# A two-layer linear-attention and MLP kernel: token layout of the tiles, store queues, a zero-padded block of W_down, and a new written-out order

## The chip, the cores and the metric

The kernel runs on one core of one Trainium2 chip. A core has five engines with an instruction queue each: TensorE (PE in the profile, its weight loads PEld), VectorE (DVE), ScalarE (ACT), GpSimd (POOL) and SyncE (SP). SP and ACT issue the kernel's DMAs. The metric is the device time of one execution in microseconds (us); a kernel's time is the median of its runs. Before the change that is 368.83 us, from 3 runs between 368.44 and 368.85.

## The reference, cut to what matters

Tokens S = 2048, width D = 512, H = 32 heads of Dh = 16, MLP width F = 1376, all bfloat16. The same weights serve both layers.

```python
def A(x):                       # linear attention, hedgehog feature maps
    q, k, v = split(x @ wqkv)   # each (H, S, Dh)
    pq, pk = q @ w_phi, k @ w_phi                          # 16x16 per head
    phi_q = concat(softmax(pq), softmax(-pq))              # 32 features
    phi_k = concat(softmax(pk), softmax(-pk))
    kv, z = sum_s phi_k * v, sum_s phi_k                   # per head
    o = (phi_q @ kv) / (phi_q . z + 1e-6)
    return o @ wo

def B(x):                       # gated MLP
    gate, up = x @ W_gate, x @ W_up                        # 512 -> 1376
    return (relu(gate) * up) @ W_down                      # 1376 -> 512

x = x + A(layernorm(x)); x = x + B(layernorm(x))
x = x + A(layernorm(x)); x = x + B(layernorm(x))
```

The sum over s in kv and z runs over all 2048 tokens, so no query of a layer can be finished before the last key of that layer.

## The kernel before, in words

**Tiling.** The 2048 tokens are 16 tiles of 128 tokens, one token to a partition. x stays in on-chip memory for the whole kernel, in four buffers X[c] of four tiles each (tile t is `X[t // C][:, t % C]`, C = 4). Lines 284 and 285 say which tokens make a tile:

```python
    xv = xf.rearrange("(c p i) d -> c p i d", c=C, i=C)
    ov = of.rearrange("(c p i) d -> c p i d", c=C, i=C)
```

A chunk of 512 tokens makes four tiles, and tile i of the chunk takes every fourth token, i, i + 4, and so on. Four tokens that follow each other in DRAM lie in one partition, one in each tile. Tiles 0 to 3 are loaded one by one, tiles 4 to 15 in pairs (`load_x`, L351 for all loads of the head); a load of a pair reads two adjacent tokens, 2 KB, for each partition.

**The operations.** The body of the kernel emits nothing at once. It makes 1855 operations with `op(engine, cost, due, emit, ...)`; an operation is a handful of instructions on one engine. They are numbered as they are made. Four tables at the head of the file decide the rest, and nothing is planned when the kernel is built (costs and due times are left over and unused): ORDER is the order in which the operations are emitted, a permutation of 0 to 1854, and so the order of each engine's queue; PLACE has a bit for each operation that exists in two versions (`alt`), and a 1 takes the other version (another engine, mostly); SLOTS gives the buffer of each operation that takes one; IDLE is the number of dummy matmuls ahead of each of the first five TensorE operations (`idle`, L437), beside nine of them in an operation of their own at the start. The engines run their queues on their own and wait for each other through semaphores.

**Head.** Operation 0 preloads ScalarE's table of functions, 1 loads tile 0 of x, 2 and 3 load the halves of W_v, 4 to 6 tiles 1 to 3, 7 w_phi, 8 and 9 the halves of W_k, 10 to 15 the pairs of tiles 4-5 to 14-15; 16 makes the identity matrix and the constant ones on POOL (`first_constants`). The load of x's tile 0, of w_phi and of the four weight halves can be issued by SP or ACT (`load`); W_q's halves are operations 322 and 323 on SP (L850). W_k is folded with w_phi into Wk2 before it is used: its four blocks are transposed by TensorE ("turn", L463), copied to SBUF (wT, L443 on ACT or L444 on DVE), multiplied by the block matrix Wblk ("fold", L471; Wblk is made by L419 on POOL or DVE) and copied again (W2). W_q is transposed by DMA and folded in the same way later.

**A tile through layer one's keys.** Mean and variance on VectorE (L500, L501), ln and exp on ScalarE for the inverse deviation (L508, L510), the normed tile xn on POOL (L520 and L522) or VectorE (L524), its transpose xnTA by TensorE (L490, then a copy by ACT) for tiles 0 to 3 and by a DMA of SP (L485) for the others. Then K (L581, four matmuls of 480 columns) and V (L586, four of 512) on TensorE; from K two exponentials on ScalarE (ek, L564), their sums on VectorE (sk, L591), ln and exp of these on ScalarE (L600, L603), the feature product phi on POOL or VectorE (L551); V is copied by ACT or DVE (vext, L443/L444). Features times V, kvz (L614), accumulate over the 16 tiles in one PSUM buffer.

**Queries and attention.** When the last kvz is done, VectorE makes R and Rz of it (L626, L631). Queries run beside: Q (L641), exponentials (L564), sums (sq, L646), their product (phq, L657 and L662), a transpose by a DMA of SP (fq, L666), features times R on TensorE (erq, L677), the division (L688, L691), the transpose of the result, proj (L700), and the residual resS (L704), which is added to X in place.

**MLP.** It runs in blocks of 1, 1, 2, 4, 4 and 4 tiles. A tile is centred (xc, L720), its squares are summed (ssq, L726 on ACT or L728 on DVE), and it is transposed (xnTB). F = 1376 is ten blocks of 128 and one of FR = 96: GU (L753) computes the last 96 columns of gate and up for two tiles at once, hr (DVE) and hrT, a DMA transpose by SP (L804), bring them into h; G and Up (L777) compute the ten others, with the relu on ACT (rg, L781) and the product on DVE, directly (ru, L794) or by way of a copy on ACT (L796, then hT, L785). `down` (L817) multiplies the eleven blocks of h by W_down, 128 rows for ten of them and 96 rows for the last (`h.t[:m, ...]` and `wd[:m, ...]`); the rows 96 to 127 of h's last block are zero already, since the columns 96 to 127 of hr are set to zero at the start (`hr_zero`). resB (L824, VectorE) adds the result to X in place. In layer two the last tile is done in two parts, of 384 and 128 columns. In layer one each resB is followed by the norm and the keys of layer two for the same tile, in layer two by the store of the tile, all 17 stores by SP (L890).

**The order around the change.** In before, SP and ACT issue the loads of the head in this order (@ACT marks those of ACT): x tile 0 @ACT, x 2, w_phi @ACT, W_k first half, x 1, x 4-5, W_k second half, x 3, W_v second half, W_v first half, x 6-7, x 8-9, x 12-13, W_q first half, W_q second half, then transposes and the other loads between them. The heads of the compute queues of before, with tile or block numbers:

```
ACT  x0 load, w_phi load, table, ln2, rstd2, ln0, wT0, wT1, ln1, rstd0, rstd1, xnT copy (tile 2), W2.1 ...
PE   warm, turn0, turn1, xnT2, fold1, turn2, turn3, fold0, xnT0, fold3, fold2, xnT1, V0, K0, K2, xnT3,
     K1, V2, V3, K3, V1, K4, Wq fold, K5, Wq fold, V5, kvz0 ...
SP at the end   hrT, then 13 stores: tiles 13, 3, 0, 6, 11, 1, 7, 10, 12, 8, 14, 15 (384 columns), 15 (128 columns)
```

Of the kernel before, what the change touches and what calls it, by code (L numbers as in the profile page):

```python
# [8 lines left out]
P = 128  # L9
# [3 lines left out]
F = 1376  # L13
NB = D // P
NF = 11
# [130 lines left out]
class K:  # L146
# [9 lines left out]
    "1001001010001001101010000101111000001001111100100001101100111011000011000000100000101111011100010100"  # L156
    "1001101111010010110000010110000011011001111010011101100111110011110011001111111010011101111101011001"
    "1100011011011000110101111111111101111110010101011000010100100001101000100101111100010011011001010100"
    "1010110010011111000100110101101001100101100011101100100"
)  # L160
SLOTS = (
    "0001450332111040002521331020252213134130241204554001324122142118332305232454002133223601357001146113"
    "37331110214c1029215b124e344a030f050d1609305j031g253c321b012i144h204k360a1200050401151502000212011020"
    "2400001150000020350210121400102105010002500401004005212214201851002313115213501425303231310500410142"
    "1024202011521574410443221121100401010352431312302242101240511013402460230322025003051301002510502000"
    "1042222135013132244254224011350135402481030275405k21311041150211321401210232450232222330131532542063"
    "2110112025213310385404e052f313d2459131i320j201b062b154f210c145a3509160h004d212e331g12011301020313001"
    "0124302000035011021540000124501002145001012230210000111041011030210121231001501441322200001041042225"
    "0420351321112001514214224324413412402523105223205102100110050000220551450552131532232412541321040123"
    "1130421000550542551212451342421030015034"  # L170
# [3 lines left out]
    0, 0, 0, 0, 1,  # L174
# [104 lines left out]
def kernel(  # L279
# [22 lines left out]
    def x_of(t):  # L302
        return X[t // C][:, t % C, :]
# [52 lines left out]
    def load_x(t, n, due, follow=(), eng="SP"):  # L356
        o = load(due, X[t // C][:, t % C:t % C + n, :], xv[t // C][:, t % C:t % C + n, :], n * 131072, eng, follow, t < 1)
        x_in[t:t + n] = [o] * n
# [577 lines left out]
```

## Time and profile before

| | |
|---|---|
| median of 3 runs (lowest, highest) | 368.83 us (368.44, 368.85) |
| the profiled execution | 368.89 us |
| its span, from the first instruction to the last | 367.1 us |
| instructions | 6928 |
| PE busy | 360.5 us, 98%, 2589 matmuls |
| DVE busy | 267.8 us, 73% |
| ACT busy | 188.2 us, 51% |
| POOL busy | 71.4 us, 19% |
| moved by DMA | 31.70 MB, mean 86 GB/s |

The profile is one execution, taken by the hardware profiler. Its times begin at the start of the span; 1.8 us of the execution lie around the span. In rows of instructions the first number is the start and the second the duration (both us), then the engine, the line, the operation, the tile that it writes and those it reads, shapes (partitions x elements), and in square brackets how long the engine was idle before it and what ended that wait. A row with "xN" groups N instructions that follow each other. Rows of stages have the stretch, its length, then the busy time of PE, PEld, DVE, ACT and POOL with the number of instructions, the granted TensorE clock as a share of full speed, the share of DMA engines busy, and GB/s. Engine names ending in "q" (SPq, ACTq) are the queue that issues DMAs.

### The profile page before, as it was taken

The page shows a single profiled execution, that of the slowest core. Times are in us where ns is not written, and L with a number is a line of the kernel's source. Part 1 is how long each engine was busy: PE and PEld are TensorE (multiplying, and loading weights), DVE is VectorE, ACT ScalarE, POOL GpSimd, SP SyncE. Part 2 cuts the span into 40 slices and gives each one's busy share as a digit, 9 for nine tenths or more (in the row PEclk, how much of TensorE's full clock was granted, in tenths as well). Part 3 has the DMA queues.
Part 4 walks back from the last instruction along what each step waited for, and adds up shares of the span by engine and source line. Part 5 has one row for each costly group of instructions (what it writes and reads, how often), then busy time and mean ns, then how long its engine had stood idle before and what let it go on. Part 6 is the DMA issues. An engine that isn't in the chain of part 4 may idle for free.

```text
span 367.1 us, 6928 instructions
## 1 busy us (share of the span) xinstructions
PE 360.5 (98%) x2589; PEld 199.2 (54%) x2589; DVE 267.8 (73%) x607; ACT 188.2 (51%) x530; POOL 71.4 (19%) x101
## 2 busy tenths in 40 slices
PE   8999999999999999999999999999999999999994
PEld 4445568786545444444544556776755444454442
DVE  6999999998887247958789898899756745251342
ACT  6899998361434633414883375863423441434220
POOL 6579831210010001000208363010300000000000
PEclk9999999999999999999999999999999999999999
DMA  7987776466730600041110206346652210200025
GB/s 246 214 208 203 192 163 130 90 127 134 116 71 18 131 10 3 1 100 30 29 42 3 57 4 145 45 77 147 145 119 57 63 30 0 57 2 14 0 59 173
DMA packets 92994, 31.70 MB, mean 86 GB/s; under 512 B 85184, under 2 KB 91168, under 8 KB 92960
## 3 DMA queue, kind: packets, MB, share of 16 engines
q1 hardware_dynamic: 92288, 31.11, 38.1%
q8 instruction: 20, 0.33, 0.4%
q10 hardware_dynamic: 672, 0.15, 0.2%
q14 instruction: 14, 0.11, 0.1%
HBM read 8.44 MB, written 2.10 MB: 29 GB/s over the span
## 4 chain that ended last, share of the span: by engine, by line
PE 93%; DMA 3%; DVE 2%; issue 0%; ACTq 0%; SPq 0%; ACT 0%
PE b L777 38%; PE b L817 21%; PE b L700 8%; PE b L641 7%; PE b L586 6%; PE b L581 6%; PE b L753 3%; PE q L614 2%; PE q L677 2%; DMA X<-in_A_x_dram 2%; DMA wf<-in_A_w_phi_dram 1%; DVE bstA L500 1%; PE b L490 1%; DVE sk L591 1%; DVE X L824 0%
## 5 line engine op out<-in xcount | busy, mean ns | idle before, releaser
L777 PE MATMUL b<-xnTB,wgu 128*128 128x512 bf16 (+2 forms) x960 | 150.7, 308 | 0.0
L777 PEld LDWEIGHTS <-wgu 128*128 128x128 bf16 x960 | 80.3, 98 | 57.4 <-issue 0.2
L781 ACT ACTIVATE gu<-b 128x512 bf16<-128x512 f32 (+1 forms) x82 | 47.9, 589 | 100.0 <-PE b L777 93.6
L817 PE MATMUL b<-wd,hT 128*128 128x512 bf16 (+3 forms) x363 | 84.1, 372 | 0.0
L564 ACT ACTIVATE ek<-b 128x480 bf16<-128x480 f32 x128 | 68.2, 585 | 11.4 <-PE b L641 7.0
L794 DVE TENSOR_TENSOR hT<-gu,b 128x512 bf16<-128x512 bf16 (+1 forms) x53 | 35.1, 663 | 36.3 <-PE b L777 19.8
L551 POOL TENSOR_TENSOR ek<-ek 128x480 bf16<-128x480 bf16 x40 | 39.2, 1008 | 94.2 <-ACT ek L603 93.9
L817 PEld LDWEIGHTS <-hT 128*128 128x128 bf16 (+1 forms) x363 | 34.5, 98 | 37.4
L591 DVE TENSOR_REDUCE sk<-ek 128x64 f32<-128x960 bf16 x32 | 36.1, 1143 | 1.8 <-ACT ek L564 0.9
L646 DVE TENSOR_REDUCE sq<-ek 128x64 f32<-128x960 bf16 x32 | 36.4, 1144 | 0.0
L662 POOL TENSOR_TENSOR ek<-ek 128x480 bf16<-128x480 bf16 x18 | 18.3, 1020 | 87.2 <-DVE ek L657 56.6
L700 PE MATMUL b<-wo,oT 128*128 128x512 bf16 x128 | 31.4, 379 | 0.0
L586 PE MATMUL b<-wv,xnTA 128*128 128x512 bf16 x128 | 31.4, 379 | 0.0
L824 DVE SCALAR_TENSOR_TENSOR X<-b,rsB,X 128x512 bf16<-128x512 f32 (+2 forms) x33 | 23.8, 727 | 9.0 <-PE b L817 8.6
L581 PE MATMUL b<-Wk,xnTA 128*128 128x480 bf16 x128 | 30.2, 366 | 0.0
L641 PE MATMUL b<-Wq,xnTA 128*128 128x480 bf16 x128 | 30.1, 365 | 0.0
L691 DVE TENSOR_TENSOR o<-q,rd 128x512 bf16<-128x512 f32 x32 | 22.0, 689 | 10.0 <-ACT rd L688 9.7
L785 DVE TENSOR_TENSOR hT<-gu 128x512 bf16<-128x512 bf16 x29 | 12.1, 421 | 21.0 <-ACT gu L796 21.0
L796 ACT CAST gu<-b 128x512 bf16<-128x512 f32 x29 | 17.0, 586 | 16.2 <-PE b L777 15.4
L704 DVE SCALAR_TENSOR_TENSOR X<-b,X 128x512 bf16<-128x512 f32 x32 | 22.0, 686 | 3.5 <-PE b L700 3.3
L500 DVE BATCH_NORM_STATS2 bstA<-X 128x6 f32<-128x512 bf16 x32 | 21.3, 682 | 2.1 <-DMA X<-in_A_x_dram 2.0
L700 PEld LDWEIGHTS <-oT 128*128 128x128 bf16 x128 | 12.2, 98 | 13.2
(77 smaller groups left out, 328.8 us busy)
## 6 DMA issues: line engine op xcount, KB each, us to landing
out_dram<-X SPq DMA_DIRECT2D x15, 128.0 KB, 2.2
X<-in_A_x_dram SPq DMA_DIRECT2D x6, 256.0 KB, 4.7
wgu<-in_B_W_gate_dram SPq DMA_DIRECT2D x4, 344.0 KB, 3.4
wgu<-in_B_W_up_dram SPq DMA_DIRECT2D x4, 344.0 KB, 4.0
wd<-in_B_W_down_dram SPq DMA_DIRECT2D x5, 256.0 KB, 3.9
hT<-in_A_wqkv_dram SPq DMA_DIRECT2D x4, 256.0 KB, 5.3
wv<-in_A_wqkv_dram SPq DMA_DIRECT2D x2, 256.0 KB, 4.5
wo<-in_A_wo_dram SPq DMA_DIRECT2D x4, 128.0 KB, 4.0
```

Source lines behind the costliest of these rows:

```text
L551: e.tensor_tensor(out=v[:, :, 0:DF, :], in0=v[:, :, 0:DF, :], in1=spread(ek, v, n), op=Alu.mult)
L564: nc.scalar.activation(out=pairs(ek, s)[:, :, 0:DF, :], in_=ps.t[:, 0:FW].rearrange("p (b f h) -> p b f h", h=2, f=DF), func=AF.Exp, scale ...
L581: k = op("PE", mm(4, FW), due, lambda: [nc.tensor.matmul(kp.t[:, 0:FW], lhsT=xnTA[c][:, i, b, :], rhs=Wk2[:, b, :], start=(b == 0), stop=( ...
L586: v = op("PE", mm(4, 512), due_v, lambda: [nc.tensor.matmul(vp.t[:], lhsT=xnTA[c][:, i, b, :], rhs=wv[:, b, :], start=(b == 0), stop=(b == ...
L591: a = op("DVE", SUM16, due, lambda: nc.vector.tensor_reduce(out=sk.t[:, row, :].rearrange("p (b h) -> p b h", h=2), in_=summed(pairs(ek)), ...
L641: q = op("PE", mm(4, FW), due, lambda: [nc.tensor.matmul(qp.t[:, 0:FW], lhsT=xnTA[c][:, i, b, :], rhs=Wq2[:, b, :], start=(b == 0), stop=( ...
L646: a = op("DVE", SUM16, due, lambda: nc.vector.tensor_reduce(out=sq.t[:].rearrange("p (b h) -> p b h", h=2), in_=summed(pairs(ek)), axis=AX ...
L700: a = op("PE", mm(4, 512), due + 3, lambda j=j, yp=yp: [nc.tensor.matmul(yp.t[:], lhsT=oT.t[:, j, b, :], rhs=wo[:, b, :], start=(b == 0), ...
L777: nc.tensor.matmul(ps.t[:, q * W:(q + 1) * W].rearrange("p (i t) -> p i t", t=P), lhsT=wgu[:, s, b, g * P:(g + 1) * P], rhs=xT.t[:, 0:n, b ...
L781: nc.scalar.activation(out=gu.t[:, 0, 0:cols], in_=gp.t[:, 0:cols], func=AF.Relu)
L794: nc.vector.tensor_tensor(out=h.t[:, f0 * W:f0 * W + cols], in0=gu.t[:, 0, 0:cols], in1=up.t[:, 0:cols], op=Alu.mult)
L817: nc.tensor.matmul(yp.t[:, 0:c1 - c0], lhsT=h.t[:m, f * W + i * P:f * W + (i + 1) * P], rhs=wd[:m, f, c0:c1], start=(f == 0), stop=(f == N ...
```

## The change

Four edits of the body, and new tables.

```diff
-    xv = xf.rearrange("(c p i) d -> c p i d", c=C, i=C)
-    ov = of.rearrange("(c p i) d -> c p i d", c=C, i=C)
+    xv = xf.rearrange("(t p) d -> p t d", p=P)
+    ov = of.rearrange("(t p) d -> p t d", p=P)
...
-        o = load(due, X[t // C][:, t % C:t % C + n, :], xv[t // C][:, t % C:t % C + n, :], n * 131072, eng, follow, t < 1)
+        o = load(due, X[t // C][:, t % C:t % C + n, :], xv[:, t:t + n, :], n * 131072, eng, follow, t < 1)
...
     def first_constants():
         make_identity(nc, ident[:])
+        nc.gpsimd.memset(wd[FR:P, NF - 1, :], 0.0)
         for i in ONES:
...
                         for f in range(lo, hi):
-                            m = min(P, F - f * P)
-                            nc.tensor.matmul(yp.t[:, 0:c1 - c0], lhsT=h.t[:m, f * W + i * P:f * W + (i + 1) * P],
-                                             rhs=wd[:m, f, c0:c1], start=(f == 0), stop=(f == NF - 1))
+                            nc.tensor.matmul(yp.t[:, 0:c1 - c0], lhsT=h.t[:, f * W + i * P:f * W + (i + 1) * P],
+                                             rhs=wd[:, f, c0:c1], start=(f == 0), stop=(f == NF - 1))
...
-                    op("SP", (460, 1700), e0, lambda t=t, c0=c0, c1=c1: nc.sync.dma_start(
-                        out=ov[t // C][:, t % C, c0:c1], in_=x_of(t)[:, c0:c1]), [a], name="store",
-                       move=256 * (c1 - c0) / RATE)
+                    ways = [(e, (460, 1700), lambda q=q, t=t, c0=c0, c1=c1: q.dma_start(
+                        out=ov[:, t, c0:c1], in_=x_of(t)[:, c0:c1]), False)
+                            for e, q in (("SP", nc.sync), ("ACT", nc.scalar))]
+                    op(*ways[0][:2], e0, ways[0][2], [a], name="store", move=256 * (c1 - c0) / RATE, alt=ways[1])
...
 IDLE = (
-    0, 0, 0, 0, 1,
+    0, 1, 0, 0, 1,
 )
...
 ORDER = (
-    1, 16, 5, 29, 7, 8, 25, 0, 4, 20, 19, 28, 10, 9, 6, 82, 3, 83, 46, 2, 21, 11, 18, 30, 26, 22, 47, 32, 12, 17, 84,
+    1, 16, 5, 29, 7, 4, 22, 21, 18, 20, 25, 0, 8, 10, 28, 9, 2, 82, 6, 46, 14, 83, 64, 11, 47, 12, 30, 26, 19, 27, 32,
...
```

A tile is now 128 adjacent tokens, so the tokens of a pair lie 128 KB apart in DRAM, and a load of a pair reads a run of 1 KB for each token. W_down's last block is padded to 128 rows with zeros, set once by POOL, and every matmul of `down` is 128 rows deep. A store can go by SP or by ACT, as PLACE says.

PLACE has 17 bits more, for the stores, and nearly all of PLACE, SLOTS and ORDER is new. Decoded, these are the differences that bear on the steps:

- *Loads.* Order of issue: x 0 @ACT, x 2, w_phi @ACT, x 1, W_k first half, x 4-5, W_k second half, W_v first half, x 3, x 12-13, x 6-7, x 8-9, W_q first half, W_q second half, W_v second half @ACT, x 10-11, a transpose, x 14-15, then the rest.
- *ACT's head.* x0 load, w_phi load, table, ln2, rstd2, load of W_v's second half, ln0, ln1, rstd0, rstd1, wT1, wT0, wT3, W2.1, ln4, W2.3, rstd4, W2.2, xnT copy (tile 0), vext2 and so on.
- *PE's head.* warm, turn0, turn1, xnT2, turn3, turn2, fold1, xnT0, fold0, fold3, xnT1, fold2, V2, K2, K0, V1, K1, xnT3, V0, K3, V3, K5, V5, Wq fold, K4, Wq fold, V4, Wq fold, K12, K13, Wq fold, kvz0 and so on. One more dummy matmul stands ahead of turn0.
- *Engines.* Wblk moves from POOL to DVE. Copies of V: 20 to 27 of 32 on ACT. Halves of phi in layer one and two: 40 to 36 on POOL. Squares: 17 to 20 of 32 on ACT. Divisions by reciprocal on DVE: 17 to 20 of 32. Direct products (ru) on DVE: 53 to 54.
- *Layer borders.* Between layer one's first proj and the transpose behind it stand two Q on TensorE, where one stood; between the last kvz of layer two and its first erq two Q as well, where one stood.
- *Stores.* 17 on SP become 8 on SP and 9 on ACT. At the end SP has hrT, then the stores of tiles 11, 7, 10, 13 and of the last 128 columns of tile 15; ACT has those of tiles 2, 5, 8, 4, 1, 12, 14, 6 and of the first 384 columns of tile 15, between relus.

More of the change, by code (lines that the diff above doesn't have):

```diff
@@ L155 @@
 PLACE = (
[L156 to L159, printed above, removed]
+    "1011000011111011000010000110111100001000111010100011101110001011000111000000100000111011011101011000"
@@ L160 @@
+    "1000000000100110111100101111111100010001111100001101100010110100000001111101011000101101001101101101"
+    "1111010000100011100111111011110000000000111101110000011101111100101010001100100000011000000000000000"
+    "101100010110101100011111101111111101000110110000010000010011011111010110"
 )
 SLOTS = (
-    "0001450332111040002521331020252213134130241204554001324122142118332305232454002133223601357001146113"
-    "37331110214c1029215b124e344a030f050d1609305j031g253c321b012i144h204k360a1200050401151502000212011020"
@@ L164 @@
[L164 to L168, printed above, removed]
@@ L169 @@
-    "0420351321112001514214224324413412402523105223205102100110050000220551450552131532232412541321040123"
-    "1130421000550542551212451342421030015034"
+    "0001430523113142102412212020050015332300452115404302023332500138010015412044214311225600217423116040"
+    "35233101034a101c3159035d121b244h050g160a303d031i045k214c323e155f302j36192100030501101002000203011020"
+    "4300001112000020500210123100102152010000120505005002023012203152202515115011321410523033210300400141"
+    "0304223221210172133832121151140411210042142022352032450151221435450333014450000622012343100100011002"
@@ L171 @@
+    "100224224413501301115020215325110k2422512121j1134150111231140511300211202312030440131352121442030474"
+    "4033213240402110025020b130a210h004g352k125d332c162c312b304i040h331i061e210g103f054912011524020511001"
+    "0104502000241011021410000105501002141001010420210022504041050022150012111301421400551252011002033055"
+    "1432240042011101012113304113325401220213022104503342020021030520541511540252452111520231222110542115"
+    "1000101542231041300040212412330221143105"
 )
```

176 rows, old and new, of the table ORDER are left out of this document.

## The prediction, made before the changed kernel was run

> **What bounds the kernel.** I read the page's busy shares first, then the chain that ended last, then the starts of TensorE's matmuls in order of time, looking for places where one starts later than the one before it allows.
>
> ```profile
> span 367.1 us, 6928 instructions
> PE 360.5 (98%) x2589; PEld 199.2 (54%) x2589; DVE 267.8 (73%) x607; ACT 188.2 (51%) x530; POOL 71.4 (19%) x101
> PE 93%; DMA 3%; DVE 2%; issue 0%; ACTq 0%; SPq 0%; ACT 0%
> 20.09 0.86 PE b L586 x4
> 27.14 0.81 PE b L641 x4
> ```
>
> TensorE is busy for 98% of the span and makes 93% of the chain. Four matmuls of 512 columns take 0.86 us in the chain of waits, four of 480 columns 0.81, so an interval between matmuls that is longer than this is a stall. A reordering can't shorten the matmuls; it can only change three things: when TensorE's unbroken work begins, the few stalls inside it, and what follows the last matmul. This is the start of the work on TensorE and on the other engines around it:
>
> ```profile
> 8.82 0.40 PE L490 MATMUL b<-ident,xn 128*128 128x128 bf16 x4
> 9.06 1.03 PE L586 MATMUL b<-wv,xnTA 128*128 128x512 bf16 x4
> 0.00:20.00 20.00, 18.03 (x123) 9.05 (x124) 16.61 (x44) 15.11 (x44) 11.72 (x38) 1.00 0.95 229
> 20.00:60.00 40.00, 40.00 (x361) 22.74 (x359) 38.56 (x71) 39.05 (x120) 26.54 (x31) 1.00 0.75 184
> ```
>
> Until 9.06 TensorE does transposes and folds in snatches; from the first V at 9.06 it runs nearly without a break. The stage rows (engines in the order PE, PEld, DVE, ACT, POOL) show that from 20 to 60 us VectorE (38.56 of 40) and ScalarE (39.05 of 40) are nearly as full as TensorE: a lag made before 20 us isn't easily won back there, and an earlier TensorE would soon wait for them.
>
> The stalls inside the work are few. Three can be named:
>
> ```profile
> 18.12 1.03 PE L586 MATMUL b<-wv,xnTA 128*128 128x512 bf16 x4
> 19.45 0.43 PE L614 MATMUL q<-vext,ek 128*128 128x65 bf16 x8 [0.30 <-DVE ek L551]
> 55.78 0.97 PE L641 MATMUL b<-Wq,xnTA 128*128 128x480 bf16 x4
> 56.72 0.40 PE L490 MATMUL b<-ident,xn 128*128 128x128 bf16 x4
> 225.62 0.97 PE L641 MATMUL b<-Wq,xnTA 128*128 128x480 bf16 x4
> 226.67 0.41 PE L677 MATMUL q<-R,fq 128*128 128x68 bf16 x8
> ```
>
> 18.12 + 0.86 is 18.98, and the next starts at 19.45: 0.47 lost, on a phi product of VectorE. 55.78 + 0.81 is 56.59 against 56.72: 0.13 lost. 225.62 + 0.81 is 226.43 against 226.67: 0.24 lost, on R of the second layer. This is the end:
>
> ```profile
> 361.94 0.97 DVE L824 SCALAR_TENSOR_TENSOR X<-b,rsB,X 128x384 bf16<-128x384 f32 x2 [0.39 <-PE b L817]
> 363.75 0.41 SPq L890 DMA_DIRECT2D out_dram<-X  x1
> out_dram<-X SPq DMA_DIRECT2D x1, 32.0 KB, 2.3
> 357.69 6.47 SPq L890 DMA_DIRECT2D out_dram<-X  x13
> ```
>
> VectorE is done at 361.94 + 0.97 = 362.91, but the last store is issued at 363.75, since SyncE is working off 13 stores one after the other (6.47 us for 13: 0.50 each). It lands 2.3 us later, and the clearing of semaphores ends the span.
>
> **The change, part by part. ScalarE is held in the head.** The new order puts the load of W_v's second half, now issued by ScalarE, right behind the norm of tile 2. It is the fifteenth DMA of the order. What a late DMA waits for can be read in the head of before:
>
> ```profile
> 2.16 0.43 SPq L351 DMA_DIRECT2D X<-in_A_x_dram  x1
> X<-in_A_x_dram SPq DMA_DIRECT2D x1, 256.0 KB, 4.0
> 2.63 0.43 SPq L351 DMA_DIRECT2D hT<-in_A_wqkv_dram  x1
> hT<-in_A_wqkv_dram SPq DMA_DIRECT2D x1, 256.0 KB, 4.3
> 6.18 0.38 SPq L850 DMA_DIRECT2D hT<-in_A_wqkv_dram  x1
> 6.94 0.38 SPq L850 DMA_DIRECT2D hT<-in_A_wqkv_dram  x1
> ```
>
> The sixth and seventh DMA of the order of before start at 2.16 and 2.63 and land at 6.16 and 6.93; the fourteenth and fifteenth, which need no data, are issued at 6.18 and 6.94. So each DMA waits for the landing of the one eight before it. In the new order the seventh is W_k's second half again, with the same loads ahead of it, so it lands at about 6.93 again. On SyncE such a wait held only further loads. On ScalarE it holds, in order, the norms of tiles 0 and 1 (L508, L510) and the copies of W_k's transposes (L443). Their times before, with POOL's part of the norms:
>
> ```profile
> 4.53 0.20 ACT L510 ACTIVATE rsA<-lnA 128x1 f32<-128x1 f32 x1
> 5.21 0.20 ACT L508 ACTIVATE lnA<-mvA 128x1 f32<-128x1 f32 x1 [0.48 <-DVE mvA L501]
> 5.32 1.05 ACT L443 COPY hT<-b 128x512 bf16<-128x512 bf16 x2
> 7.71 0.19 POOL L520 TENSOR_SCALAR nm<-mvA 128x1 f32<-128x1 f32 x1
> 8.00 0.77 POOL L522 TENSOR_SCALAR xn<-X,nm,rsA 128x512 bf16<-128x512 bf16 x1
> L351 ACTq DMA_DIRECT2D wf<-in_A_w_phi_dram x1: 459/459/459, 1.2 to 1.2; - x1
> ```
>
> After: ScalarE ends the norm of tile 2 at about 4.7, or a little later, stands to 6.93, issues for 0.46, and goes on at 7.4; of these 2.7 us it idled 0.48 in before as well. Two ln and two exp take it to 7.8; POOL scales tile 0 from 7.9 to 8.7 and tile 1 (0.19 + 0.10 + 0.77 later) to 9.7; the copies of W_k end at 8.4, 8.9 and 9.4. TensorE's order wants tile 1's transpose ahead of the last fold and of the first V: 9.75, then two groups of 0.22 each, and V starts at 10.2, not 9.06. W_v's second half arrives at the same time: 128 KB on each queue together landed 2.8 us after issue,
>
> ```profile
> X<-in_A_x_dram ACTq DMA_DIRECT2D x1, 128.0 KB, 2.8
> 6.00:7.50 1.50, 1.13 (x19) 0.88 (x16) 1.31 (x3) 1.50 (x6) 1.40 (x3) 1.00 1.09 383
> 8.50:10.00 1.50, 1.50 (x13) 0.88 (x14) 1.44 (x5) 1.47 (x6) 1.39 (x4) 1.00 1.00 343
> ```
>
> and twice as much beside as much again adds 256 KB at 383 GB/s, 0.7 us (estimate): 6.95 + 3.5 = 10.4 at worst. **+1.1 us.** Bounds: 0 if ScalarE isn't held, +2.2 if its whole hold (2.7 - 0.48) reaches TensorE.
>
> **Stalls that go.** The 0.47 at 18.98 goes: both halves of the first phi are now on POOL, and TensorE comes to it 4.0 us later: 1.1 late, with three more groups of K or V and two folds (2.9 us) ahead of it. VectorE is late next, at R of layer 0. The 0.13 at 56.6 goes, since two Q instead of one now lie between the first proj and the transpose that stalled, and the 0.24 at 226.4 goes in the same way: two Q, 1.6 us, between the last kvz and the first product with R. **-0.84**, bounded by 0 and -0.84, and against it up to +0.8 for stalls that I don't see in the new order.
>
> **Stores.** Nine of 17 go to ScalarE, and SyncE ends with five, only one of the last two among them. Both queues are then empty at 362.91, so the last store is issued 0.8 us earlier: **-0.8**, between 0 and -1.0. On ScalarE a store waits for VectorE's residual with relus behind it, and TensorE's down products wait for these. In that stage ScalarE is busy for a small part,
>
> ```profile
> 340.00:367.10 27.10, 22.52 (x121) 11.02 (x118) 9.79 (x21) 3.88 (x7) 0.00 (x0) 0.99 0.25 79
> ```
>
> 3.88 of 27.1 us, so nine issues of 0.46 fit; without that cover a relu held by 0.5 us would cost TensorE as much. SyncE's transposes of hr and o lose what stood ahead of them. I take 0.
>
> **Layout.** Loads of two tiles now read runs of 1 KB where they read 2 KB. In the stage 6.0 to 7.5, where W_k, X3 and W_v come in 1 KB runs, the DMAs moved 383 GB/s; from 8.5 to 10, with 2 KB runs, 343. I take 0, and keep one tenth of a 256 KB load, 0.07 us, either way. The Trainium skill, page "DMA: Bandwidth & Descriptors", section "Why small descriptors are slow (HBM only)", speaks against it: each packet costs about three cycles beside one per 32 bytes. By it (an estimate from that page) two runs of 1 KB cost 70 cycles for 67, 4% or 0.03 us a load; the rows above go the other way.
>
> **Padding.**
>
> ```profile
> L817 PE MATMUL b<-wd,hT 128*128 128x512 bf16 x310 | 77.2, 379 | 0.0
> L817 PE MATMUL b<-wd,hT 96*128 96x512 bf16 x31 | 11.8, 381 | 0.0
> L396 POOL MEMSET ek<- 128x32 bf16 x12 | 0.8, 127 | 0.0
> 4.36 0.19 POOL L520 TENSOR_SCALAR nm<-mvA 128x1 f32<-128x1 f32 x1 [2.33 <-DVE mvA L501]
> 5.69 1.01 POOL L419 TENSOR_TENSOR Wblk<-wd,Mf 128x480 bf16<-128x480 bf16 x1
> ```
>
> 96 rows take 381 ns and 128 take 379, so the wider matmuls are free. The memset of 32 rows by 512 on POOL lies between these bounds: 0.13 us, and 16 times that, 2 us; I take 0.5. POOL waited 2.33 us for tile 2's mean at that point, which covers it. W_blk moves from POOL (1.01 us) to VectorE, while ScalarE is held; the extra dummy matmul ends before W_k lands; vext and squares move from VectorE to ScalarE, lnd and rden back. Each is off the path by these rows: 0, or up to 0.3 us in the stage where both are full.
>
> **Sum.** The profiled execution took 368.89 us, 1.8 more than its span. 368.89 + 1.1 - 0.84 - 0.8 = 368.35; the median of before is 0.06 below the profiled run, so I forecast **368.3**.
>
> **Rivals.** *ScalarE isn't held* (the wait is met sooner, or other work fills it): V starts at 9.1, and the sum is 367.2. But then VectorE, 96% full from 20 to 60, gives back some 0.3: 367.5. For it: the copies still have room until 6.93, when W_k's second half lands. Against it: the two issue times above fall on landings to 0.02 us.
>
> *The hold is kept whole*: ScalarE is 98% full from 20 to 60 and loses 2.2 us in the head. It decides if the exponentials, not TensorE, pace the first keys: then the head costs +2.2, the 0.47 isn't saved, and the sum is 368.83 + 2.2 - 0.37 - 0.8 = 369.9, slower. For it: that stage row. Against it: in before ScalarE idled in the head too, 15.11 of 20, and TensorE has queries to put between.
>
> *The stores bring nothing*: a store from ScalarE lands as much later as it is issued earlier. Then 369.1. Against it: X's load from that queue took 2.8 us, and SyncE's beside it as long.
>
> **Chances.** Forecast 0.46 (its own range 367.7 to 368.9), not held 0.22, held whole 0.22, stores nothing 0.10. A difference of 0.2%, 0.74 us, is about what a measurement of this kernel can tell from none: under 368.09 is faster, over 369.57 slower. Of the forecast 0.18 lies below and 0.28 between. Faster 0.18 + 0.22 = 0.40, within 0.28 + 0.10 = 0.38, slower 0.22. The range from 367.3 to 369.8 leaves out half of the slow case and a part of the fast one.
>
> **What would show it.** ScalarE's issue of W_v at 6.9 with nothing behind it until 7.4, the first matmul of L586 at 10.2, no wait at the first kvz, no gap ahead of the first L677 of layer 2, five stores or fewer in SyncE's last run, and the last issue within 0.1 us of VectorE's end. It is wrong if the first V starts near 9, if TensorE has new gaps of over 0.3 us after 20 us, or if the span's end lies more than 4.2 us behind the last matmul.

## The result, and the profile after

The changed kernel takes 372.05 us (median of 5 runs, 371.13 to 372.62), the kernel before 368.67 (368.44 to 368.85) beside it: a ratio of 1.0091, 95% interval 1.0072 to 1.0109. It is slower by 3.4 us, where 368.3 was forecast. The page of the changed kernel begins so:

```profile
span 370.2 us, 6929 instructions
PE 362.7 (98%) x2590; PEld 200.3 (54%) x2590; DVE 266.6 (72%) x604; ACT 190.1 (51%) x534; POOL 67.1 (18%) x97
```

The shares are those of before: TensorE is still the bound, and no share of the whole span tells where 3.1 us of span have come from. So I read the stages of the head. First the changed kernel, then the same three stretches of the kernel before (length, busy time of PE, PEld, DVE, ACT, POOL, granted TensorE clock, DMA share, GB/s):

```profile
7.40:9.20 1.80, 0.27 (x5) 0.09 (x2) 1.06 (x5) 1.02 (x6) 0.43 (x1) 1.00 1.05 339
11.20:13.30 2.10, 0.46 (x3) 0.10 (x1) 2.10 (x6) 1.11 (x3) 1.07 (x2) 1.00 0.54 174
13.30:16.50 3.20, 3.19 (x9) 1.13 (x9) 1.91 (x7) 1.94 (x5) 0.59 (x1) 0.51 0.77 193
```

```profile
7.40:9.20 1.80, 1.80 (x25) 1.24 (x23) 1.80 (x8) 1.79 (x6) 1.60 (x5) 1.00 0.96 310
11.20:13.30 2.10, 2.10 (x15) 1.12 (x14) 2.10 (x8) 1.35 (x3) 0.00 (x0) 1.00 1.31 172
13.30:16.50 3.20, 3.20 (x17) 1.46 (x16) 3.20 (x9) 2.81 (x10) 1.38 (x4) 1.00 1.13 134
```

TensorE stands still in two stretches where it was full before, and in a third it is "busy" for 3.19 of 3.20 us but makes 9 matmuls instead of 17: its clock is 0.51 there. The matmuls of the changed kernel in order of time name the waits:

```profile
7.05 0.62 PE L464 MATMUL b<-ident,hT 128*128 128x128 bf16 x8
9.23 0.38 PE L472 MATMUL b<-Wblk,hT 128*128 128x120 bf16 x4 [1.57 <-ACT hT L444]
...
11.07 0.59 PE L587 MATMUL b<-wv,xnTA 128*128 128x512 bf16 x2
13.31 0.99 PE L587 MATMUL b<-wv,xnTA 128*128 128x512 bf16 x2 [1.65 <-DMA wv<-in_A_wqkv_dram]
14.10 3.11 PE L582 MATMUL b<-Wk,xnTA 128*128 128x480 bf16 x8
17.05 1.03 PE L587 MATMUL b<-wv,xnTA 128*128 128x512 bf16 x4
```

The first wait is for ScalarE's copy of a transposed block of W_k. The first V then starts at 11.07, not 9.06: +2.01. Its last two matmuls need W_v's second half and start at 13.31, where they could have started at 11.07 + 2 x 0.216 = 11.50: +1.81. From there TensorE runs at half clock: 14.10 - 13.31 = 0.79 for two matmuls instead of 0.43 (+0.36), and 17.05 - 14.10 = 2.95 for two K instead of 1.62 (+1.33). Together +5.5 us by 17.05.

ScalarE in that time:

```profile
4.76 0.20 ACT L511 ACTIVATE rsA<-lnA 128x1 f32<-128x1 f32 x1
7.75 0.38 ACTq L351 DMA_DIRECT2D wv<-in_A_wqkv_dram  x1
8.18 0.30 ACT L509 ACTIVATE lnA<-mvA 128x1 f32<-128x1 f32 x2 [3.21 <-DVE hT L445]
8.61 1.54 ACT L444 COPY hT<-b 128x512 bf16<-128x512 bf16 x3
```

After the norm of tile 2 it does nothing until it can issue the load at 7.75, and the next norm follows right behind. The bracket names a copy of VectorE, which this ln doesn't need; what stands ahead of it in its own queue is the load. The landings (KB, us from issue) explain the 7.75 and the 13.31:

```profile
wv<-in_A_wqkv_dram SPq DMA_DIRECT2D x1, 256.0 KB, 4.6
wv<-in_A_wqkv_dram ACTq DMA_DIRECT2D x1, 256.0 KB, 5.5
```

SyncE issued the first half at 3.15, so it landed at 7.75: that is the landing that ScalarE waited for. The second half was issued then and landed at 7.75 + 5.5 = 13.25. The landing that the forecast had in mind, that of W_k's second half at 2.64 + 4.4 = 7.04, let another load through, SyncE's of x's tiles 10 and 11, although it stands behind this one in the order:

```profile
7.09 0.47 SPq L351 DMA_DIRECT2D X<-in_A_x_dram  x1
```

What follows the head is better than before. The places of the three stalls of the forecast, in the changed kernel:

```profile
27.07 0.37 PE L472 MATMUL b<-Wblk,hT 128*128 128x120 bf16 x4
27.29 0.42 PE L615 MATMUL q<-vext,ek 128*128 128x65 bf16 x8
...
55.64 1.78 PE L642 MATMUL b<-Wq,xnTA 128*128 128x480 bf16 x8
57.26 0.39 PE L491 MATMUL b<-ident,o 128*128 128x128 bf16 x4
...
229.84 1.78 PE L642 MATMUL b<-Wq,xnTA 128*128 128x480 bf16 x8
231.46 0.42 PE L678 MATMUL q<-R,fq 128*128 128x68 bf16 x8
```

Each second row begins where the first allows it: two Q take 2 x 0.81 = 1.62, and 55.64 + 1.62 = 57.26, 229.84 + 1.62 = 231.46. The 0.47, 0.13 and 0.24 us of before are gone. The end:

```profile
365.78 1.43 PE L817 MATMUL b<-wd,hT 128*128 128x384 bf16 x15
366.30 1.66 SPq L890 DMA_DIRECT2D out_dram<-X  x2
366.63 0.96 DVE L824 SCALAR_TENSOR_TENSOR X<-b,rsB,X 128x384 bf16<-128x384 f32 x2 [0.36 <-PE b L817]
out_dram<-X SPq DMA_DIRECT2D x1, 32.0 KB, 1.5
```

SyncE's last two issues end at 367.96, so the last (0.33 us long) begins at 367.63; VectorE ends at 367.59. The last store no longer waits for its queue, and it lands in 1.5 us instead of 2.3. From TensorE's end (365.78 + 1.43 = 367.21) to the span's end are 3.02 us. In the kernel before TensorE's last group was this one,

```profile
360.77 1.76 PE L817 MATMUL b<-wd,hT 128*128 128x384 bf16 x17
```

it ended at 362.52 (the row's times are rounded), and 4.59 us followed (the spans end at 370.23 and 367.11). The account: +5.5 in the head, -0.84 for the stalls, -1.57 behind the last matmul make +3.1, and the spans differ by 370.2 - 367.1 = 3.1.

### The profile page after: what moved, and what is told of

It reads as the page before. It is cut to its first block, busy times and chain, and to the rows that moved or that the text cites. A ratio compares the mean times of both kernels' runs of the same rounds, so it can differ in the third digit from the quotient of the medians.

```text
span 370.2 us, 6929 instructions
## 1 busy us (share of the span) xinstructions
PE 362.7 (98%) x2590; PEld 200.3 (54%) x2590; DVE 266.6 (72%) x604; ACT 190.1 (51%) x534; POOL 67.1 (18%) x97
## 4 chain that ended last, share of the span: by engine, by line
PE 93%; DMA 4%; DVE 1%; SPq 1%; ACT 1%; issue 0%
PE b L778 37%; PE b L817 19%; PE b L587 7%; PE b L701 7%; PE b L582 7%; PE b L642 7%; PE b L754 3%; DMA wv<-in_A_wqkv_dram 3%; PE q L615 2%; PE q L678 2%; DMA oT<-o 1%; PE b L491 1%; SPq L351 1%; ACT ek L565 1%; DVE sk L592 0%; DVE X L824 0%
## 5 line engine op out<-in xcount | busy, mean ns | idle before, releaser
L778 PE MATMUL b<-xnTB,wgu 128*128 128x512 bf16 (+2 forms) x960 | 152.8, 308 | 0.0
L817 PE MATMUL b<-wd,hT 128*128 128x512 bf16 (+2 forms) x363 | 84.5, 372 | 0.0
L817 PEld LDWEIGHTS <-hT 128*128 128x128 bf16 x363 | 34.5, 98 | 37.8
L795 DVE TENSOR_TENSOR hT<-gu,b 128x512 bf16<-128x512 bf16 (+1 forms) x54 | 35.7, 666 | 24.1 <-PE b L778 16.6
L552 POOL TENSOR_TENSOR ek<-ek 128x480 bf16<-128x480 bf16 x36 | 35.4, 1010 | 89.3 <-DVE xn L721 65.2
L663 POOL TENSOR_TENSOR ek<-ek 128x480 bf16<-128x480 bf16 x18 | 18.2, 1018 | 98.7 <-DVE ek L658 73.5
L587 PE MATMUL b<-wv,xnTA 128*128 128x512 bf16 x128 | 32.2, 382 | 1.6 <-DMA wv<-in_A_wqkv_dram 1.6
L701 PE MATMUL b<-wo,oT 128*128 128x512 bf16 x128 | 32.4, 379 | 0.1
L582 PE MATMUL b<-Wk,xnTA 128*128 128x480 bf16 x128 | 31.8, 378 | 0.0
L797 ACT CAST gu<-b 128x512 bf16<-128x512 f32 (+1 forms) x28 | 16.1, 573 | 17.3 <-PE b L778 17.3
L786 DVE TENSOR_TENSOR hT<-gu 128x512 bf16<-128x512 bf16 (+1 forms) x28 | 11.9, 429 | 15.5 <-ACT gu L797 15.5
L582 PEld LDWEIGHTS <-xnTA 128*128 128x128 bf16 x128 | 12.6, 101 | 13.8 <-issue 2.1
```

Of the source, the lines that this page charges most:

```text
L552: e.tensor_tensor(out=v[:, :, 0:DF, :], in0=v[:, :, 0:DF, :], in1=spread(ek, v, n), op=Alu.mult)
L582: k = op("PE", mm(4, FW), due, lambda: [nc.tensor.matmul(kp.t[:, 0:FW], lhsT=xnTA[c][:, i, b, :], rhs=Wk2[:, b, :], start=(b == 0), stop=( ...
L587: v = op("PE", mm(4, 512), due_v, lambda: [nc.tensor.matmul(vp.t[:], lhsT=xnTA[c][:, i, b, :], rhs=wv[:, b, :], start=(b == 0), stop=(b == ...
L701: a = op("PE", mm(4, 512), due + 3, lambda j=j, yp=yp: [nc.tensor.matmul(yp.t[:], lhsT=oT.t[:, j, b, :], rhs=wo[:, b, :], start=(b == 0), ...
L778: nc.tensor.matmul(ps.t[:, q * W:(q + 1) * W].rearrange("p (i t) -> p i t", t=P), lhsT=wgu[:, s, b, g * P:(g + 1) * P], rhs=xT.t[:, 0:n, b ...
L795: nc.vector.tensor_tensor(out=h.t[:, f0 * W:f0 * W + cols], in0=gu.t[:, 0, 0:cols], in1=up.t[:, 0:cols], op=Alu.mult)
```

## The experiments

Theory A: the whole loss is made in the head, by the late landing of W_v's second half, the hold of ScalarE, and the clock that falls while TensorE waits. Theory B: the rest of the new order costs. Within A it is open which of hold and landing sets the time (A2 and A1). Each kernel ran beside the kernel before on the same chip; experiments 1 to 4, 5 to 8 and 9 to 11 share these runs of before (27, 33 and 11 of them).

### 1. W_v's second half early, by SyncE

```diff
 ORDER (changed kernel; 3 is W_v's second half, 2 its first)
-    ..., 28, 9, 2, 82, 6, ... 17, 84, 85, 86, 3, 48, ...
+    ..., 28, 9, 2, 3, 82, 6, ... 17, 84, 85, 86, 48, ...
 PLACE: the bit of operation 3 from 1 (ACT) to 0 (SP)
```

> The changed kernel, but W_v's second half is issued by SyncE right behind its first half, so it is the ninth load and no load stands in ScalarE's queue behind the norm of tile 2. Theory A (the loss is made in the head: W_v lands at 13.2 us behind seven other loads, ScalarE is held to 8.2, and TensorE then runs at half clock until 16.5): first V near 9.1, granted clock 1.00 from 13 to 16.5; 1.73 + 1.81 + 1.69 = 5.2 us go from 372.05, of which up to 1 us may come back as other waits: 366.8 to 367.8. Theory B (the rest of the new order costs, in the stage from 20 to 60 us where VectorE and ScalarE are full): 369.5 or more.

Measured: 367.73 us (12 runs, 366.91 to 369.37) against 368.83, ratio 0.9967 (0.9951 to 0.9983). TensorE in its profiled execution:

```profile
9.42 0.60 PE L587 MATMUL b<-wv,xnTA 128*128 128x512 bf16 x2
10.21 0.59 PE L587 MATMUL b<-wv,xnTA 128*128 128x512 bf16 x2 [0.20 <-DMA wv<-in_A_wqkv_dram]
...
13.30:16.50 3.20, 3.07 (x18) 1.41 (x17) 3.20 (x11) 2.84 (x10) 2.02 (x5) 1.00 1.20 190
```

V starts at 9.42, the clock stays at 1.00, and moving this one load turns a slower kernel into one that beats the kernel before. Theory B falls: the rest of the new order is not slower. Of the 5.5 us of the head 4.3 come back. In the profiled execution, the slowest of the twelve, V starts 0.36 us later than in before, and TensorE waits 0.83 us at 54.8 for a transposed block of features and 0.34 at 19.2 for a transposed block of W_q; in the changed kernel it has neither wait. So some waits return when TensorE is earlier; how large they are in the other executions no trace shows.

### 2. Late, but by SyncE: no hold

```diff
 PLACE: the bit of operation 3 from 1 (ACT) to 0 (SP); ORDER as in the changed kernel
```

> The changed kernel, with W_v's second half at its late place in the order, but issued by SyncE: ScalarE is not held, the load still stands behind seven others. Theory A1 (the late landing sets the time, the hold is covered by it): folds end near 9.3, V still waits to 12.5 or 13.3, time 371.3 to 372.3. Theory A2 (the hold of ScalarE sets it, as the forecast had it): the first V is complete by 10.5, time 368 to 369.5.

Measured: 370.33 (10 runs, 369.30 to 371.88), ratio 1.0043 (1.0025 to 1.0061). TensorE's first V:

```profile
9.46 0.59 PE L587 MATMUL b<-wv,xnTA 128*128 128x512 bf16 x2
12.20 0.59 PE L587 MATMUL b<-wv,xnTA 128*128 128x512 bf16 x2 [2.15 <-DMA wv<-in_A_wqkv_dram]
```

Without the hold V starts at 9.46 again, but the load, issued at 6.69, takes 5.5 us and V waits to 12.20. The landing alone makes the kernel slower than before. Its time lies between the two ranges: above A2's 368 to 369.5 and below A1's 371.3, so the landing is not the whole loss either.

### 3. The hold alone

```diff
-        first_x(t, 2)(())
+        first_x(t, 2, "ACT" if t == 10 else "SP")(())
 ORDER: 3 right behind 2 (by SP), and 13 (x's tiles 10 and 11) where 3 stood
```

> The changed kernel, with W_v's second half issued early by SyncE and the load of x's tiles 10 and 11 in its late place on ScalarE: the hold alone, without the late weights. Theory A1: ScalarE stands from 4.9 to about 7.0 to 7.8, the first fold waits some 1.0 to 1.7 us as in the changed kernel, V does not wait, the clock stays at 1.00: 367.5 to 369.3. Theory A2 (the hold sets it): 371 to 372.3.

Measured: 369.32 (12 runs, 368.37 to 370.56), ratio 1.0009 (0.9995 to 1.0023), 0.02 above A1's range. The first fold and the first V:

```profile
9.81 0.38 PE L472 MATMUL b<-Wblk,hT 128*128 128x120 bf16 x4 [2.10 <-ACT hT L444]
...
12.20 1.69 PE L587 MATMUL b<-wv,xnTA 128*128 128x512 bf16 x4
```

ScalarE stands from 5.4 to 8.33 here, since the load was issued later than in the changed kernel. A1's clock of 1.00 is missed as well: the first four matmuls of V take 1.69 us instead of 1.03, and the granted clock was 0.50 from 11.2 to 13.3; three of the twelve executions show such a fall. The hold alone costs 1.6 us against the first experiment and would have cancelled the change's gain.

### 4. The waits filled with dummy matmuls

```diff
 IDLE = (
-    0, 1, 0, 0, 1,
+    0, 1, 0, 0, 1, 0, 7, 0, 0, 0, 0, 0, 10,
 )
```

> The changed kernel with 7 dummy matmuls ahead of the first fold and 10 ahead of the first V, which fill TensorE's two waits; the loads are as in the changed kernel. If the half clock from 13.3 to 16.5 us comes from TensorE having stood still: the clock stays at 1.00, 1.69 us go, and 0.43 come back since the first two matmuls of V now run behind the dummies: 370.8 (370.2 to 371.5). If the clock has another cause, the dummies only cost: 372.3 to 372.8.

Measured: 371.28 (5 runs, 370.90 to 371.85), ratio 1.0058 (1.0039 to 1.0077), in the range for a clock that falls because TensorE stood still. In the stretch in which the changed kernel had a clock of 0.51 it is now 1.00:

```profile
14.11 1.02 PE L587 MATMUL b<-wv,xnTA 128*128 128x512 bf16 x4
...
13.30:16.50 3.20, 3.20 (x17) 1.50 (x16) 3.20 (x10) 1.29 (x5) 0.19 (x1) 1.00 0.49 100
```

So the half clock does come from TensorE's standing still. But in this profile the load is issued at 8.52, not 7.75, and the first V begins at 14.11, so the time can't be set against the changed kernel's alone; the mean granted clock of every execution says more (below).

### 5 and 6. The stores

Experiment 5 is the kernel of experiment 1 with all stores by SyncE (17 bits of PLACE at 0). Experiment 6 is the kernel before, with the second, fourth, ... twelfth of its last 13 stores given to ScalarE (the new `ways` of the diff, with the old layout).

> The kernel of the first experiment (W_v early), with all 17 stores issued by SyncE at the same places of the order. If the two queues are worth what the forecast gave them: the last five stores are issued one after the other, the last at 0.4 to 0.8 us behind VectorE's end, and the span ends 0.5 to 1.0 us later: 368.2 to 368.8. If the stores bring nothing: 367.7. If what the two traces differ by behind the last matmul (1.57 us) is all due to the queues: 369.3.

> The kernel before, with 6 of its last 13 stores moved to ScalarE, which has no work left behind its last copy; nothing else is changed. Forecast's step: the last store is issued 0.8 us earlier: 368.0. If stores on two queues also land sooner: 367.3. If the stores bring nothing: 368.8. Work ahead of 350 us is the same instruction for instruction.

Measured: experiment 5 takes 368.25 (12 runs, 367.16 to 369.82), ratio 0.9982 (0.9966 to 0.9998); experiment 6 takes 367.46 (10 runs, 367.05 to 368.36) against 368.90, ratio 0.9960 (0.9948 to 0.9973). The end of experiment 6, then that of experiment 5:

```profile
358.56 5.59 SPq L890 DMA_DIRECT2D out_dram<-X  x7
355.25 8.56 ACTq L890 DMA_DIRECT2D out_dram<-X  x6
out_dram<-X SPq DMA_DIRECT2D x1, 32.0 KB, 1.7
```

```profile
355.27 8.23 SPq L890 DMA_DIRECT2D out_dram<-X  x9
out_dram<-X SPq DMA_DIRECT2D x1, 32.0 KB, 1.5
```

In experiment 6 the six stores of ScalarE stand behind its last copy, so they hold nothing, and 1.4 us are gained by them alone, twice the forecast's step: the last store is issued at VectorE's end (0.8), and it lands 0.6 sooner. The profiled execution of 6 is the slowest of the ten, but behind VectorE's end 2.8 us follow in it, and 4.2 in before.

In the new order the second queue is worth less. The medians of 1 and 5 differ by 0.5, about as expected, though their ranges overlap and the difference isn't clear of the scatter. The traces give 0.4: from TensorE's last matmul to the span's end are 3.03 us in experiment 1 (367.59 - 364.56) and 3.43 in experiment 5 (365.73 - 362.30). So of the 1.57 us that the end of the changed kernel is shorter, the second queue makes about 0.4, and about 1.2 stay with all stores on SyncE, where the new order leaves fewer stores for the end. In experiment 5 the last store is issued 0.5 us behind VectorE's end and still lands in 1.5 us, so a sooner landing doesn't need the second queue; what makes it was not tested.

### 7 and 8. Layout and padding alone

Experiment 7 is the kernel before with the four lines of the layout, experiment 8 the kernel before with the memset and the 128-row matmuls.

> The kernel before with the new layout alone: tiles of 128 adjacent tokens, so loads of pairs in runs of 1 KB. Forecast's step: 0, within 0.3: 368.5 to 369.1. If short runs cost 4% of each load and the head waits for them: 369.1 to 369.4.

> The kernel before with the padding alone: the memset of 32 rows by 512 on POOL, and 128 rows in each matmul of the last block. Forecast's step: 0, the memset about 0.5 us inside POOL's wait: 368.6 to 369.0. If the memset delays the first norm on POOL: up to 369.4. If the wider matmuls let TensorE's weight loads run more evenly: below 368.5.

Measured: 368.76 (12 runs), ratio 1.0000 (0.9988 to 1.0011), and 368.81 (12 runs), ratio 0.9997 (0.9983 to 1.0011). Neither makes a difference clear of the scatter: by the intervals each is worth 0.6 us at most.

### 9. W_k ahead of tile 1 as well

```diff
 ORDER (kernel of experiment 1; 8 is W_k's first half, 4 is tile 1)
-    1, 16, 5, 29, 7, 4, 22, 21, 18, 20, 25, 0, 8, 10, ...
+    1, 16, 5, 29, 7, 8, 4, 22, 21, 18, 20, 25, 0, 10, ...
```

> The kernel of the first experiment, with W_k's first half issued ahead of tile 1 of x, as in the kernel before. There TensorE waited 1.21 us for W_k behind the dummies, 0.28 in the kernel before. If W_k's landing paces the head: 0.4 to 0.9 us less than the first experiment, 366.8 to 367.3. If tile 1's norm, now later, paces it: 367.5 to 368.2.

Measured: 367.40 (5 runs, 367.23 to 367.93) against 368.76, ratio 0.9962 (0.9950 to 0.9974). It falls between the two ranges, 0.3 below experiment 1, less than the two medians can resolve. With experiment 6 it is the best version found; each is 1.4 us under the kernel before.

### 10. The late load in the kernel before

```diff
 ORDER (kernel before; 85 is the norm of tile 2, 14 x's tiles 12 and 13, 322 and 323 W_q)
-    ..., 84, 85, 86, ...
+    ..., 84, 85, 14, 322, 323, 3, 86, ...
 PLACE: the bit of operation 3 from 0 (SP) to 1 (ACT)
```

> The kernel before, with W_v's second half issued late by ScalarE behind the norm of tile 2 (and the loads of tiles 12 to 15's first pair and of W_q put ahead of it), so that it is the fifteenth load as in the change; everything else is the kernel before. Theory A (late landing and hold make the loss, whatever the rest of the order): V waits until about 13, the clock falls, 4.2 us more than before, 372.0 to 374.0. Theory B (the new order can't bear it, the old one could): below 370.5.

Measured: 372.01 (5 runs, 371.66 to 373.16) against 368.76, ratio 1.0090 (1.0076 to 1.0103), as in the change. ScalarE and TensorE:

```profile
7.57 0.37 ACTq L351 DMA_DIRECT2D wv<-in_A_wqkv_dram  x1
7.99 0.20 ACT L508 ACTIVATE lnA<-mvA 128x1 f32<-128x1 f32 x1 [3.16 <-DVE bstA L500]
```

```profile
9.21 0.58 PE L471 MATMUL b<-Wblk,hT 128*128 128x120 bf16 x4 [2.75 <-ACT hT L443]
7.40:9.20 1.80, 0.00 (x0) 0.00 (x0) 1.02 (x4) 1.21 (x5) 0.00 (x0) 0.72 1.02 375
9.20:11.20 2.00, 1.99 (x20) 1.99 (x21) 0.52 (x2) 2.00 (x9) 1.59 (x3) 0.50 1.07 367
11.20:13.30 2.10, 1.93 (x16) 1.60 (x16) 2.10 (x6) 1.40 (x5) 1.19 (x4) 0.50 0.21 70
13.30:16.50 3.20, 3.15 (x15) 1.48 (x15) 3.20 (x10) 1.84 (x4) 0.96 (x2) 0.73 0.62 132
```

Much the same edit makes the same loss in the old order: a hold until 7.57, a fold that waits for a copy, and a clock of 0.50. Putting this load late, by ScalarE and with three others now ahead of it, is sufficient. The shares differ from those of the changed kernel: the load landed at 7.57 + 5.1 = 12.67 and the first V began at 12.49, so in this profile, the slowest of the five, the hold and the clock make the loss and the landing is covered by them.

### 11. Fewer loads ahead of it

```diff
 ORDER (changed kernel; 322 and 323 are W_q's halves)
-    ..., 32, 322, 65, 118, 323, 17, 84, 85, 86, 3, 48, ...
+    ..., 32, 65, 118, 17, 84, 85, 86, 3, 322, 323, 48, ...
```

> The changed kernel, with W_q's two loads put behind W_v's second half, which stays on ScalarE behind the norm of tile 2: it is now the thirteenth load, so it waits for the landing of the fifth or sixth (5.6 to 6.2 us), and five loads are outstanding ahead of it, not seven. If loads of both queues are served in the order of their issue: it lands 2 x 0.75 us earlier than in the changed kernel, at 11.2 to 11.8, and the time is 369.2 to 370.5. If the two queues share the engines half and half: it lands by 9.3, and the time is 367.7 to 368.7.

Measured: 370.63 (6 runs, 370.04 to 371.72), ratio 1.0049 (1.0034 to 1.0064), in neither range. It tells nothing on its question: the queues of all five engines, and the loads for which each load waits, came out as in the changed kernel, instruction for instruction. The load went again when W_v's first half landed, at 3.14 + 5.0 = 8.14, so the place in ORDER alone doesn't say which landing a load waits for. It is a second sample of the changed kernel, 1.4 us below the first, and that asked for an explanation.

The mean granted clock of each execution gives it. Of the 11 executions of these queues (5 of the changed kernel and 6 here), three had a clock of 1.00 and took 370.04, 370.31 and 370.71; eight had 0.990 to 0.995 and took 370.56 to 372.62, median 371.7. Experiment 2 splits in the same way (six at 0.999 or above, median 370.2; four at 0.994, median 371.4), and experiment 3 (nine at 0.999 or above, median 369.2; three at 0.995, 370.4 to 370.6). An episode of half clock is worth 1.2 to 1.4 us and comes in some executions and not in others; with the dummies of experiment 4 all five had 1.00. At full clock the medians are 367.6 for experiment 1 (11 executions), 369.2 with the hold (+1.6), 370.2 with the late landing (+2.6), 370.3 with both (+2.7, three executions): while V waits for its weights, the hold costs nearly nothing more. That is A1, with the clock as a third part.

## Why the prediction was wrong, point by point

**The bound** was right: TensorE, and what counts is when its unbroken work begins.

**The hold of ScalarE** was right in kind and too small. It went on at 8.18, not 7.4, since the load took its turn behind the landing at 7.75 and not behind W_k's at 7.04, which went to SyncE's load of tiles 10 and 11. The first V began 2.0 us later instead of 1.1; experiment 3 prices the hold at 1.6. Both lie in the bound of 2.2.

**The step that failed** is "W_v's second half arrives at the same time", with "10.4 at worst". It landed at 13.25. I took a load of 128 KB on an empty machine (2.8 us) and added only 256 KB for what moves beside it. But a load that had to wait for the landing of the eighth before it has seven others outstanding: here 6.5 loads of 256 KB, 1.7 MB, which at the 343 GB/s of the forecast's own row take 5.0 us, and its own 256 KB 0.8 more. A row of the kernel before says it outright; W_q's second half, the fifteenth load, issued at 6.94:

```profile
hT<-in_A_wqkv_dram SPq DMA_DIRECT2D x1, 256.0 KB, 6.3
```

I had used that row's issue time and not its landing. Experiments 1 and 2 price the landing at 2.6 us.

**The clock** was no term of the sum. Once TensorE had stood twice it ran at half clock for 3.4 us: +1.7 in the profile, 1.2 to 1.4 in the runs.

**The stalls that go** did go, all three, for the sum given (0.84). **The stores** term was -0.8, and the end got shorter by 1.57, outside my bound of -1.0: I counted the sooner issue (0.8) and not the faster landing. I put it down to the two queues; by experiment 5 most of it is the new order. **Layout and padding** were nothing that shows, by experiments 7 and 8, as costed. My comparison of 383 GB/s with 343 was no evidence for it, though: with runs of 2 KB as in before, experiment 8 moved 376 GB/s from 8.5 to 10.

**The signs.** The issue at 6.9 and the first V at 10.2 did not come out (7.75 and 11.07). The others did: no wait at the first kvz, no gap ahead of the first L678 of layer two (L677 in before), five stores in SyncE's last run, the last issue 0.04 us behind VectorE's end, no wait of TensorE over 0.3 us after 20 us, and the span's end 3.0 us behind the last matmul. None of them looked at the landing, and so the step that failed had no sign of its own.

**The rivals.** "The hold is kept whole" had the sign and some of the size (369.9), but not the mechanism: it needed exponentials on a full ScalarE to pace the keys, and experiment 2 is slower than before without any hold. "The stores bring nothing" is out by experiment 6. "ScalarE isn't held" is out by the issue at 7.75, though its 367.5 is near what the kernel does once the load is moved (367.73).

With its three terms as measured (+5.5 in the head where I had +1.1, -0.84, -1.57) the forecast's own sum gives 368.89 + 3.1 = 372.0.

## What to carry to other kernels

Before a load is put late in a row of loads, find a load of the kernel at hand that already stands as late, and take its landing time as the price: the bytes outstanding ahead of it divided by the rate, whatever queue it is issued from (W_v's second half took 5.5 us from ScalarE's queue and from SyncE's). A load that may have to wait for an earlier one doesn't belong in the queue of an engine that has work for others behind it; at the end of the kernel, where that engine has nothing left, the same queue is free, and moving six stores there was worth 1.4 us with no other edit, in an order that left 13 stores for the end. Price a wait of TensorE near its start at more than its length, since the clock can fall with it.

## What the runs showed of the hardware

**Two queues, one line.** The load that ScalarE issued at 7.75 moved nothing for 3 us: its first packet is of 10.86. The DMA queues (q1 is SyncE's, q10 ScalarE's: packets, MB, share of 16 engines) from 10.0 to 10.5, 10.5 to 11.0 and 11.5 to 12.0 us:

```profile
q1 hardware_dynamic: 184, 0.18, 109.6%
...
q1 hardware_dynamic: 185, 0.18, 107.1%
q10 hardware_dynamic: 2, 0.00, 1.3%
...
q10 hardware_dynamic: 132, 0.13, 81.5%
q1 hardware_dynamic: 43, 0.04, 25.4%
```

ScalarE's packets begin when SyncE's earlier loads are running out. The Trainium skill, page "DMA: Bandwidth & Descriptors", section "Queues, rings and completion order", says that each DMA engine takes turns, packet by packet, between the queues that it has work for. By that rule, if ScalarE's packets stood ready from 7.75 on, the load would have shared the engines half and half, and by the forecast's sum it would have landed at about 7.75 + 3.5 = 11.3 (an estimate); it landed at 13.25, and the measurement decides. Whether the packets stood ready, and what held them back, no run here shows; experiment 11 was meant to vary it and did not.

**The clock fell after short waits.** TensorE stood for 1.57 and 1.65 us, with work between, and ran at 0.51 from 13.3 to 16.5. In experiment 10 it stood for 2.75 us at a stretch; by the rows there (0.72, 0.50, 0.50, 0.73) the clock fell at about 8.2, while TensorE still stood, and rose at about 15.0. The half clock lasted 3.4 us in the changed kernel (13.4 to 16.8), in experiment 2 (13.2 to 16.6), in experiment 3 (10.1 to 13.5) and in experiment 11 (11.1 to 14.5), and 6.8, twice that, in experiment 10. It need not begin at a wait: in experiment 2 the only long wait was over at 12.20, and in experiment 11 TensorE was at work from 9.63 on. In the 3.4 us before each of the five falls TensorE had matmuls for 1.1 to 1.8 us; how little is enough for a fall was not tested.

The Trainium skill, page "TensorE: Matmul & The Clock Gate", section "Part 1: The HAM clock gate", gives an idle window of about 3.4 us for the fall to half and says that the window runs freely. The fall to half and the length agree, and the free window would fit that it came in 8 of 11 executions of the same queues; but no stretch without matmuls was as long as 3.4 us here, so a shorter one is enough.
